# One tile for each PSUM bank of the sums and the scratch, and eight weight blocks halved through PSUM before chunk 1

## The chip, the cores and the metric

The kernel runs on one core of a Trainium2 chip. The metric is the device time of one execution in microseconds (us). The kernel before took 1044.96 us (median of 3 runs, 1044.9 to 1045.19).

## The reference, cut to what matters

Two stages follow each other. The first is a causal convolution over seven taps whose weights are a softmax over the taps, one set for each token and head:

```
w = exp(weight_gen - max(weight_gen)); w = w / (sum(w) + 1e-9)        # [4, 4096, 8, 7]
att[b, s, h, g] = sum over k of w[b, s, h, k] * x_pad[b, s + k, h, g]   # x padded by 6 rows, 8 heads of 24
```

The second is a feed-forward block on the 16384 tokens of 192 numbers:

```
h = att @ w_in                   # [16384, 192] @ [192, 2048]
g = maximum(0.01 * h, h)
out = g @ w_out                  # [16384, 2048] @ [2048, 192]
```

## The kernel before, in words

The tokens are worked in 32 chunks of 512 (four rows of 128 partitions). POOL (GpSimd) does the convolution of a chunk ahead of its use, in 13 multiplications and additions (`conv_ops`, L359 and L363). DVE (VectorE) finds each token's largest value and a power of two for it (`scale_tokens`, L458 to L201), POOL scales by it (L464), and the result is split into a half-precision upper half (ACT, L470) and lower half (POOL, L474). Four DVE transposes (`squares`, L483), a DMA to memory and four back (L490, L500) lay the tokens out as `xx`, the operand of the first product.

A chunk takes eight steps (`step`). In each, TensorE (PE) forms two 128-wide blocks of h (`mm1`, L525, three passes: upper by upper, lower by upper, upper by lower). ACT applies the leak (L531) and takes the upper half `gh` (L545), and DVE takes the lower half `gl` (L546). PE then forms the second product (`mm2_pass`, L571) in two visits: the half of the partitions that goes to one pairing of rows in the same step as the next blocks (`mm2_first`), the other half a step later (`mm2_second`). The blocks of h are numbered n = 0 to 511; step q makes n = 2q and 2q + 1, and PE uses them in step q + 1. The second step of a chunk has no first visit, so the third has four blocks.

PSUM has eight banks. Four go to the blocks of h (`ps_h`). The other four are two tiles of two banks each, tags `o0` and `o1`: in chunks 1 to 31 they are the sums `po`. In chunk 0 and in the first two steps of chunk 1 the tile `o0` is `po0`, the sums of chunk 0 (which are formed in full precision by `mm2_whole`, L611), and `o1` is `spares`, a scratch area that is handed out half by half (`spare`).

The weights arrive in another form, are read and rounded in the beginning, and then have to be scaled and halved in 16 blocks (8 of `w_in`, 8 of `w_out`). There are two ways. Through PSUM: DVE scales into a scratch bank (`v`, L241), ACT copies the upper half (`h`, L249), DVE subtracts (`l`, L253). Straight: ACT scales from SBUF into the upper half (`H`, L258), and DVE scales and subtracts in one instruction on two SBUF operands (`L`, L264). Before, six blocks go through PSUM in the opening, four more through PSUM in steps 8 and 9, and six straight, one in each of steps 10 to 15.

The string `START` is the order written out by hand for the opening, one letter for each piece of work: `f` is a step of chunk 0, `e` one block of its second product, `1`, `2` and `3` the scales of the weights, `D` the sum and division of the softmax for chunks 2 and 3, `y`, `Y`, `X`, `R` the squares and their way through memory, and `v`, `h`, `l`, `H`, `L` the halving. Each engine runs its instructions in the order in which they are issued. DMAs are issued by SP's queue, in order as well. A wait is set by tiles: an instruction that writes a tile waits for those that still read it, whichever part they read.

Of the kernel before, what the change touches and what calls it, by code (L numbers as in the profile page):

```python
# [8 lines left out]
F32 = mybir.dt.float32  # L9
# [5 lines left out]
ALU = mybir.AluOpType  # L15
# [42 lines left out]
    "rWmrWmMppf"  # L58
    "rWmrWmpWmpNeeeef"
    "EBCVmmmmf"  # L60
    "e1De2eyY3eXvhvhlevhlevhlRvhlfvhll"
)


# [1 line left out]
def conv_attention_moe_kernel(  # L66
# [237 lines left out]
    def grouped(q, s):  # L304
        return wt[q][:, s, :].rearrange("p r (h k) -> p (r h) k", k=K)
# [239 lines left out]
        nc.scalar.copy(out=h, in_=t)  # L545
        nc.vector.tensor_tensor(out=l, in0=t, in1=h, op=ALU.subtract)  # L546

    po = [None, None]

    def new_sums():  # L550

        for i in range(2):
            po[i] = ps_o.tile([P, J // 2, TOK], F32, tag=f"o{i}", name="po")

    count = dict(mm2=0)
    after = mybir.DependencyInfo(mybir.DependencyClass.Sync, mybir.DependencyReason.DATA)
# [4 lines left out]
    def mm2_pass(ns, i, told=None):  # L561

        rows = ROWS_OF[::1 if count["mm2"] % 2 else -1]
        for n in ns:
            f = n % NF
            for g, d in ((g_h, 2 * D), (g_l, D)):
                for u, s in enumerate(HALVES):
                    j = rows[(i + u * HALF) % J]  # L570
                    ins = nc.tensor.matmul(  # L571
                        out=po[j // HALF][:, j % HALF, 0:d],
                        lhsT=g[n][s, j * P:(j + 1) * P], rhs=wo[s, f, 0:d],
                        start=(f == 0 and i < HALF and g is g_h),
                        stop=(f == NF - 1 and i >= HALF and g is g_l),
                        skip_group_check=True,
                    ).ins
                    if told is not None:
                        tc.add_manual_dep(ins, told.name, after, reason="rows left")
                        told = None  # L580
        return ins
# [24 lines left out]
    def mm2_whole(ns):  # L606

        for n in ns:
            f = n % NF
            for j in range(J):  # L610
                nc.tensor.matmul(  # L611
                    out=po0[:, j // 2, j % 2 * D:(j % 2 + 1) * D],
                    lhsT=g_h[n][:, j * P:(j + 1) * P], rhs=value((f // 2, OUT))[:, f % 2],
                    start=(f == 0 and j % 2 == 0), stop=(f == NF - 1 and j % 2 == 1),
                    skip_group_check=True,
                )
            del g_h[n]

    def evacuate_whole(c):

        r = row_of(c)
        for k in range(2):
            ot = op.tile([P, HALF, D], F32, tag="ot", name="ot", bufs=2)
            v = po0[:, k, 0:2 * D].rearrange("p (r d) -> p r d", d=D)
            if k:
                nc.vector.tensor_copy(ot, v)
            else:
                nc.scalar.copy(out=ot, in_=v)
            nc.sync.dma_start(out=out_rows[:, r + k * HALF:r + (k + 1) * HALF, :], in_=ot)
# [11 lines left out]
    def evacuate(c, last=False):  # L641


        r = row_of(c)
        for i in range(2):
            k = i if count["mm2"] % 2 else 1 - i
            ot = op.tile([P, HALF, D], F32, tag="ot", name="ot", bufs=2)
            rx = [undo_of[c][:, k * HALF + j:k * HALF + j + 1] for j in range(HALF)]
            for j in range(HALF):
                nc.scalar.activation(  # L650
                    out=ot[:, j], in_=po[k][:, j, D:2 * D], func=AF.Copy, scale=rx[j]
                )
            for j in range(HALF):
                nc.vector.scalar_tensor_tensor(  # L654
                    out=ot[:, j], in0=po[k][:, j, 0:D], scalar=rx[j], in1=ot[:, j],
                    op0=ALU.mult, op1=ALU.add,
                )
            eng = nc.scalar if last and i == 1 else nc.sync
            eng.dma_start(out=out_rows[:, r + k * HALF:r + (k + 1) * HALF, :], in_=ot)
# [31 lines left out]
    with tc.manual_schedule():  # L691
# [44 lines left out]
        def step(q):  # L736

            c, i = divmod(q, NQ)
            if i == 0 and c in sm_q:
                load_weights(sm_q[c])  # L740
                load_rows(sm_q[c])
            if i == 1 and c in sm_q:
                softmax_max(sm_q[c])
                softmax_sub(sm_q[c], nc.gpsimd)
            begun, told = pending.pop() if pending else (None, None)
            mm1(q)
            leak(2 * q)
            if begun:
                mm2_second(begun, told)
                if begun[-1] % NF == NF - 1:  # L750
                    evacuate(begun[-1] // NF)
            split_g(2 * q)
            leak(2 * q + 1)
            split_g(2 * q + 1)
            if q == WHOLE * NQ:
                mm2_whole(range(2 * q - HOLD, 2 * q))
                evacuate_whole(c - 1)
            elif firsts(q):
                ns = firsts(q)
                pending.append((ns, tell(mm2_first(ns))))  # L760
            if c == WHOLE:
                for what in "vhlvhl" if i < 2 else "HL":
                    if done[what.lower()] < len(order):
                        prepare(what)
            if i == 0:
                feed(c + 1, 2 * K)
            if c + 1 < NCH:
                first, turned = TURNS.get(c, (1, 3))
                if i == first:
                    scale_tokens(c + 1)  # L770
                if i == first + 1:
                    split_h(c + 1)
                    split_l(c + 1, nc.gpsimd)
                if i == turned:
                    squares(c + 1, 0)
                    squares(c + 1, 1)
                if i == turned + 1:
                    put_squares(c + 1)
                if i == turned + 2:
                    get_squares(c + 1)  # L780
                if i >= first:
                    feed(c + 2, 1 if c == WHOLE and i == first else 3)
            finish_softmax(c, i)

        po0 = ps_o.tile([P, J // 2, TOK], F32, tag="o0", name="po0")
        spares = ps_o.tile([P, J // 2, TOK], F32, tag="o1", name="spares")
        turn = [0]

        def spare():
            turn[0] += 1  # L790
            if 0 not in xx:
                return po0[:, 1, 0:NW]
            return spares[:, turn[0] % 2, 0:NW]

        w0 = po0[:, 0, 0:J * HK].rearrange("p (h k) -> p h k", k=K)
        away = spares.rearrange("p a b -> p (a b)")
        parts = tiles_of_sets()
        V_G, G_G = slice(0, G0), slice(G0, J * H)
        conv0 = dict(
# [13 lines left out]
        for what in START.replace(" ", ""):  # L813
# [17 lines left out]
            elif what == "a":  # L831
                softmax_max(0, SECOND)
                softmax_sub(0, nc.gpsimd, SECOND)
                softmax_exp(0, SECOND)
            elif what == "b":
                softmax_sum(0, SECOND)
                softmax_div(0, nc.gpsimd, SECOND)
            elif what in conv0:
                run(conv0[what], 1)
            elif what == "Z":  # L840
                heat(HEAT)
            elif what == "t":
                add_transposed(added)
                added += 1
            elif what == "T":
                first_tokens()
            elif what in "123":
                weight_scales("123".index(what))
            elif what == "B":
                scale_tokens(1)  # L850
            elif what == "K":
                load_weights(1)
            elif what == "k":
                load_rows(1)
            elif what == "M":
                softmax_max(1)
            elif what == "N":
                softmax_sub(1, nc.gpsimd)
            elif what == "E":
                softmax_exp(1)  # L860
            elif what == "D":
                softmax_sum(1)
                softmax_div(1, nc.gpsimd)
            elif what == "q":
                feed(2, 1)
            elif what == "C":
                split_h(1)
            elif what == "V":
                split_l(1, nc.gpsimd)
            elif what in "yY":  # L870
                squares(1, "yY".index(what))
            elif what == "X":
                put_squares(1)
            elif what == "R":
                get_squares(1)
            elif what == "f":
                mm1(n)
                leak_out(2 * n)
                leak_out(2 * n + 1)
                n += 1  # L880
            elif what == "e":
                mm2_whole([ended])
                ended += 1
            else:
                raise ValueError(what)
# [37 lines left out]
```

## Time and profile before

| what | value |
|---|---|
| median of 3 runs | 1044.96 us |
| the profiled execution | 1044.78 us |
| its span | 1043.0 us |
| PE busy | 1029.2 us, 99% |
| POOL, ACT, DVE busy | 804.8, 661.8, 565.0 us |
| chain that ended last: PE | 93% |

The span is the time from the first to the last instruction of the execution; 1.78 us lie around it. The chain that ended last is followed back from the last instruction. Time that an engine off that chain is idle costs nothing. A wait of PE, which is busy nearly throughout, is lost time unless the work after it was late anyway. The granted clock is TensorE's, in parts of full speed (1.00 is 2.4 GHz, 0.50 is 1.2 GHz).

### The profile page before, as it was taken

To read this page: it belongs to the slowest core of one execution; us is meant where nothing else is said; L and a number is where in the kernel's file an instruction comes from. 1 tells how busy PE (TensorE), PEld (TensorE's weight loads), DVE (VectorE), ACT (ScalarE), POOL (GpSimd) and SP (SyncE) were. 2 spreads that over 40 slices of the span, in tenths; PEclk is the share of its full clock that TensorE was granted. 3 is DMA by queue.
4 is the path that set the end of the run, shared out by engine and by line. 5 is a ranking of instruction groups with operands and counts; after the bars stand their busy time and mean duration, and the time that the engine had idled before them with its cause. 6 is when DMAs were issued, how large, how long until landed. Compare 5 with 4: busy or idle time off the path is not lost.

```text
span 1043.0 us, 30077 instructions
## 1 busy us (share of the span) xinstructions
PE 1029.2 (99%) x12700; PEld 679.5 (65%) x12700; DVE 565.0 (54%) x1033; ACT 661.8 (63%) x1269; POOL 804.8 (77%) x518
## 2 busy tenths in 40 slices
PE   9979999999999999999999999999999999999998
PEld 6746666666666666666666666666666666666665
DVE  7967455454555554455454555554455454555443
ACT  6547666666666666666666666666666666666664
POOL 7878977779877779877779877779877779987600
PEclk9989999999999999999999999999999999999999
DMA  9431220323222131230323222131230323211120
GB/s 246 144 99 47 87 100 32 109 62 108 62 63 94 47 123 47 76 110 33 108 63 109 62 62 94 47 124 47 84 103 31 109 62 109 63 56 38 47 63 16
DMA packets 42373, 83.06 MB, mean 80 GB/s; under 512 B 4479, under 2 KB 35839, under 8 KB 40446
## 3 DMA queue, kind: packets, MB, share of 16 engines
q1 hardware_dynamic: 42094, 80.95, 25.6%
q8 instruction: 99, 1.62, 0.6%
q14 instruction: 36, 0.29, 0.1%
q10 hardware_dynamic: 144, 0.20, 0.0%
HBM read 56.36 MB, written 24.77 MB: 78 GB/s over the span
## 4 chain that ended last, share of the span: by engine, by line
PE 93%; POOL 3%; DVE 2%; ACT 1%; DMA 1%; issue 0%; SPq 0%; DVEq 0%; POOLq 0%
PE po L571 47%; PE hp L525 46%; POOL acc L363 1%; POOL tmp L359 1%; DMA xx<-far 0%; POOL parts L391 0%; PE po L611 0%; DVE spares L241 0%; DMA far<-sq 0%; ACT hp L531 0%; DVE sm L328 0%; DMA wt<-in_weight_gen_dram 0%; DVE sq L483 0%; DVE most L184 0%; ACT gh L545 0%
## 5 line engine op out<-in xcount | busy, mean ns | idle before, releaser
L546 DVE TENSOR_TENSOR gl<-hp,gh 128x512 f16<-128x512 f32 x496 | 335.6, 686 | 348.2 <-ACT gh L545 344.9
L571 PE MATMUL po<-wo,gh 64*128 64x384 f16 x3968 | 511.7, 323 | 6.1 <-DVE wo L253 6.1
L571 PE MATMUL po<-wo,gl 64*128 64x192 f16 x3968 | 491.2, 243 | 0.4 <-DVE gl L546 0.4
L531 ACT ACTIVATE hp<-hp 128x512 f32<-128x512 f32 x496 | 292.4, 589 | 279.8 <-PE hp L525 279.8
L525 PE MATMUL hp<-xx,wi_h 64*128 64x512 f16 x2976 | 455.8, 377 | 1.0 <-DMA xx<-far 1.0
L363 POOL TENSOR_TENSOR acc<-acc,tmp 128x768 f32<-128x768 f32 x186 | 336.2, 1808 | 14.6
L571 PEld LDWEIGHTS <-gh 64*128 64x128 f16 x3968 | 225.6, 94 | 125.8 <-issue 17.4
L545 ACT CAST gh<-hp 128x512 f16<-128x512 f32 x496 | 291.3, 587 | 15.9 <-PE po L571 1.3
L359 POOL TENSOR_TENSOR tmp<-xt,wt 128x768 f32<-128x768 f32 x186 | 287.8, 1548 | 10.0
L525 PE MATMUL hp<-xx,wi_l 64*128 64x512 f16 x1488 | 295.0, 376 | 0.0
L571 PEld LDWEIGHTS <-gl 64*128 64x128 f16 x3968 | 225.0, 94 | 23.0 <-DVE gl L546 0.8
L525 PEld LDWEIGHTS <-wi_h 64*128 64x128 f16 x2976 | 161.3, 94 | 116.7 <-DMA xx<-far 1.6
L464 POOL TENSOR_TENSOR acc<-acc,xu 128x768 f32<-128x768 f32 x31 | 45.5, 1469 | 145.2 <-DVE xu L201 145.2
L525 PEld LDWEIGHTS <-wi_l 64*128 64x128 f16 x1488 | 84.6, 94 | 76.6 <-issue 0.5
L483 DVE STREAM_TRANSPOSE sq<-split 128x384 f16<-128x384 f16 x124 | 63.8, 553 | 50.5 <-POOL split L474 50.5
L654 DVE SCALAR_TENSOR_TENSOR ot<-po,xr,ot 128x192 f32<-128x192 f32 x124 | 43.2, 410 | 59.9 <-ACT ot L650 59.9
L470 ACT CAST split<-acc 128x768 f16<-128x768 f32 x31 | 25.8, 832 | 48.2 <-POOL acc L464 48.2
L474 POOL TENSOR_TENSOR split<-acc,split 128x768 f16<-128x768 f32 x31 | 51.0, 1645 | 4.7 <-ACT split L470 4.7
L359 POOL TENSOR_TENSOR acc<-xt,wt 128x768 f32<-128x768 f32 x31 | 47.8, 1543 | 0.2
L650 ACT ACTIVATE ot<-po,xr 128x192 f32<-128x192 f32 x124 | 42.2, 421 | 2.6 <-PE po L571 2.6
L458 DVE TENSOR_REDUCE xm<-acc 128x4 f32<-128x768 f32 x31 | 29.2, 943 | 0.3 <-POOL acc L363 0.3
L611 PEld LDWEIGHTS po<-bits,g 128*128 128x128 f32 x128 | 20.6, 190 | 2.7 <-DVE bits L156 0.8
(79 smaller groups left out, 288.3 us busy)
## 6 DMA issues: line engine op xcount, KB each, us to landing
xx<-far SPq DMA_DIRECT2D x124, 192.0 KB, 3.8
xt<-in_x_dram SPq DMA_DIRECT2D x14, 1344.0 KB, 5.9
out_dram<-ot SPq DMA_DIRECT2D x63, 192.0 KB, 1.9
far<-sq SPq DMA_DIRECT2D x31, 384.0 KB, 2.3
wt<-in_weight_gen_dram SPq DMA_DIRECT2D x15, 224.0 KB, 2.6
wi_raw<-in_moe_w_in_dram SPq DMA_DIRECT2D x16, 192.0 KB, 6.4
wo_raw<-in_moe_w_out_dram SPq DMA_DIRECT2D x8, 384.0 KB, 5.7
xt<-in_x_dram SPq DMA_DIRECT2D x2, 384.0 KB, 4.3
```

The source lines that it names most:

```text
L359: eng.tensor_tensor(out=out, in0=tap(c, k), in1=wk, op=ALU.mult)
L363: eng.tensor_tensor(out=acc, in0=acc, in1=out, op=ALU.add)
L464: nc.gpsimd.tensor_tensor(out=att[c], in0=att[c], in1=up.bitcast(F32).to_broadcast([P, J, D]), op=ALU.mult)
L474: eng.tensor_tensor(out=l, in0=att.pop(c), in1=h, op=ALU.subtract)
L483: nc.vector.transpose(out=sq[c][:, v, i], in_=src[:, v])
L525: nc.tensor.matmul(out=hp[2 * q + u], lhsT=w[u][s], rhs=r[s], start=(m == 0), stop=(m == len(passes) - 1),)
L531: return nc.scalar.activation(out=hp[n], in_=hp[n], func=AF.Prelu, alpha=0.01, scale=DOWN).ins
L545: nc.scalar.copy(out=h, in_=t)
L546: nc.vector.tensor_tensor(out=l, in0=t, in1=h, op=ALU.subtract)
L571: ins = nc.tensor.matmul(out=po[j // HALF][:, j % HALF, 0:d], lhsT=g[n][s, j * P:(j + 1) * P], rhs=wo[s, f, 0:d], start=(f == 0 and i < HA ...
L650: nc.scalar.activation(out=ot[:, j], in_=po[k][:, j, D:2 * D], func=AF.Copy, scale=rx[j])
L654: nc.vector.scalar_tensor_tensor(out=ot[:, j], in0=po[k][:, j, 0:D], scalar=rx[j], in1=ot[:, j], op0=ALU.mult, op1=ALU.add,)
```

## The change

Each of the four banks `o0` to `o3` becomes a tile: four tiles of sums, two of chunk 0's sums, two of scratch. The opening halves eight blocks through PSUM, in four groups of two (`vvhhll`), and a ninth straight (`HL`); the steps of chunk 1 halve one block each, straight. The put of the squares (`X`) is issued before a block of chunk 0's second product, and two multiplications of chunk 2's convolution are issued with the letter `q`. In `D` the sum of the softmax and the addition after it go to a scratch bank, and the reciprocal reads it from there.

```diff
-    "e1De2eyY3eXvhvhlevhlevhlRvhlfvhll"
+    "e1De2eyY3Xevvhhllevvhhlle"
+    "RvvhhllfvvhhllqqHL"
...
-    po = [None, None]
+    po = [None] * J
...
-        for i in range(2):
-            po[i] = ps_o.tile([P, J // 2, TOK], F32, tag=f"o{i}", name="po")
+        for j in range(J):
+            po[j] = ps_o.tile([P, TOK], F32, tag=f"o{j}", name="po")
...
-                        out=po[j // HALF][:, j % HALF, 0:d],
+                        out=po[j][:, 0:d],
...
-                    out=ot[:, j], in_=po[k][:, j, D:2 * D], func=AF.Copy, scale=rx[j]
+                    out=ot[:, j], in_=po[k * HALF + j][:, D:2 * D], func=AF.Copy, scale=rx[j]
...
-                for what in "vhlvhl" if i < 2 else "HL":
+                for what in "HL":
...
-        po0 = ps_o.tile([P, J // 2, TOK], F32, tag="o0", name="po0")
-        spares = ps_o.tile([P, J // 2, TOK], F32, tag="o1", name="spares")
+        po0 = [ps_o.tile([P, TOK], F32, tag=f"o{k}", name="po0") for k in range(2)]
+        spares = [ps_o.tile([P, TOK], F32, tag=f"o{k}", name="spares") for k in (2, 3)]
...
-            return spares[:, turn[0] % 2, 0:NW]
+            return spares[turn[0] % 2][:, 0:NW]
...
-                softmax_sum(1)
+                m = spare()[:, 0:R * H].unsqueeze(2)
+                sm[1] = win.tile([P, R * H, 1], F32, tag="sm", name="sm")
+                nc.vector.tensor_reduce(out=m, in_=grouped(1, ALL), axis=AX.X, op=ALU.add)
+                nc.vector.tensor_scalar_add(out=m, in0=m, scalar1=1e-9)
+                nc.vector.reciprocal(out=sm[1], in_=m)
```

Three places show what moves; the lines of the changed kernel are one higher than those of before, and what `D` issues has lines of its own. The first is DVE at `D`, before (`sm` is the softmax's sum, `top` the weights' largest value):

```order
L211 TENSOR_REDUCE both<-most 128x2 [waits DVE_49]
L327 TENSOR_REDUCE sm<-wt 128x64 [waits Activation_49]
L328 TENSOR_SCALAR sm<-sm 128x64 [waits DVE_49]
L329 RECIPROCAL sm<-sm 128x64 [waits DVE_49]
L220 TENSOR_REDUCE top<-spares 1x2 [waits PE_49]
```

The same place now:

```order
L212 TENSOR_REDUCE both<-most 128x2 [waits DVE_49]
L865 TENSOR_REDUCE spares<-wt 128x64 [waits Activation_49]
L866 TENSOR_SCALAR spares<-spares 128x64 [waits DVE_49]
L867 RECIPROCAL sm<-spares 128x64 [waits DVE_49]
L221 TENSOR_REDUCE top<-spares 1x2 [waits PE_49]
```

The order stays, and the addition's operands are in PSUM. The second place is DVE behind the weights' scales, in the opening, before (`wi_l` and `wo` are lower halves):

```order
L228 TENSOR_SCALAR undo<-back 128x1
L241 TENSOR_SCALAR spares<-bits,scale 128x384 [waits DVE_49]
L241 TENSOR_SCALAR spares<-bits,scale 128x384 [waits Activation_49]
L253 TENSOR_TENSOR wi_l<-spares,wi_h 128x384 [waits Activation_49]
L241 TENSOR_SCALAR spares<-bits,scale 128x384 [waits DVE_49]
L253 TENSOR_TENSOR wi_l<-spares,wi_h 128x384 [waits Activation_49]
```

The same place now:

```order
L229 TENSOR_SCALAR undo<-back 128x1
L242 TENSOR_SCALAR spares<-bits,scale 128x384 [waits DVE_49]
L242 TENSOR_SCALAR spares<-bits,scale 128x384
L254 TENSOR_TENSOR wi_l<-spares,wi_h 128x384 [waits Activation_49] x2
L242 TENSOR_SCALAR spares<-bits,scale 128x384 [waits DVE_49] x2
L254 TENSOR_TENSOR wi_l<-spares,wi_h 128x384 [waits Activation_49]
L254 TENSOR_TENSOR wo<-spares,wo 128x2x192 [waits Activation_49]
```

The second scaling no longer waits for ACT's copy of the first, and scalings and subtractions come in twos. The third place is DVE in steps 8 and 9, from the lower halves of step 8 (`gl`) to those of step 9, before:

```order
L546 TENSOR_TENSOR gl<-hp,gh 128x512 [waits Activation_49] x2
L626 COPY ot<-po_114 128x384 [waits Activation_49]
L241 TENSOR_SCALAR spares<-bits,scale 128x384 [waits DVE_49]
L253 TENSOR_TENSOR wi_l<-spares,wi_h 128x384 [waits Activation_49]
L241 TENSOR_SCALAR spares<-bits,scale 128x384 [waits DVE_49]
L253 TENSOR_TENSOR wo<-spares,wo 128x2x192 [waits Activation_49]
L315 TENSOR_REDUCE mx<-wt 128x64 [waits DMAHW4_49]
L546 TENSOR_TENSOR gl<-hp,gh 128x512 [waits Activation_49] x2
```

The same place now, with the straight block of the opening ahead:

```order
L265 SCALAR_TENSOR_TENSOR wi_l<-bits,scale,wi_h 128x384 [waits Activation_49]
L547 TENSOR_TENSOR gl<-hp,gh 128x512 [waits Activation_49] x2
L627 COPY ot<-po_115 128x384 [waits PE_49]
L265 SCALAR_TENSOR_TENSOR wo<-bits,scale,wo 128x2x192 [waits Activation_49]
L316 TENSOR_REDUCE mx<-wt 128x64 [waits DMAHW4_49]
L547 TENSOR_TENSOR gl<-hp,gh 128x512 [waits Activation_49] x2
```

Two blocks through PSUM have become one straight block, and the copy of chunk 0's second half waits for PE alone. POOL's and SP's orders are unchanged.

## Rows read from the trace of the kernel before

**Rows 1.** Waits of PE, whole program: who waited for whom, total us, times, longest.
```profile
PE po L571 <- DVE wo L253: 6.1, 1, 6.1
PE hp L525 <- DMA xx<-far: 1.0, 1, 1.0
```
**Rows 2.** Timeline (start, us, engine, line, [idle before <-releaser]): DVE and PE, 64 to 71.
```profile
66.85 0.69 DVE L546 TENSOR_TENSOR gl<-hp,gh 128x512 f16<-128x512 f32 x1 [0.41 <-ACT gh L545]
...
70.37 0.56 DVE L253 TENSOR_TENSOR wo<-spares,wo 128x384 f16<-128x384 f32 x1 [0.54 <-ACT wo L249]
...
70.98 0.51 PE L571 MATMUL po<-wo,gh 64*128 64x384 f16 x2 [6.05 <-DVE wo L253]
```
**Rows 3.** Chain that ended last, 71 to 82: start, us, what.
```profile
70.98 3.54 PE po L571 x28
74.53 2.79 PE hp L525 x18
77.31 2.94 PE po L571 x48
80.25 1.94 PE hp L525 x18
```
**Rows 4.** Busy time by stretch, with the granted clock behind the engines.
```profile
71.00:74.30 3.30, 3.30 (x29) 2.30 (x30) 2.41 (x4) 2.03 (x4) 0.00 (x0) 0.50 0.00 0
```
**Rows 5.** Timeline at the softmax's sum and the squares of chunk 1.
```profile
43.37 1.64 POOL L474 TENSOR_TENSOR split<-acc,split 128x768 f16<-128x768 f32 x1 [0.94 <-ACT split L470]
43.41 1.65 DVE L328 TENSOR_SCALAR sm<-sm 128x64 f32<-128x64 f32 x1
...
44.36 0.38 PE L214 MATMUL spares<-ident,both 128*1 128x128 f32 x2
...
45.56 0.35 DVE L220 TENSOR_REDUCE top<-spares 1x2 f32<-1x256 f32 x1
...
45.84 1.93 DVE L483 STREAM_TRANSPOSE sq<-split 128x384 f16<-128x384 f16 x4
...
55.78 0.60 PE L525 MATMUL hp<-xx,wi_h 64*128 64x512 f16 x3 [1.05 <-DMA xx<-far]
```
**Rows 6.** Timeline of the halving through PSUM on DVE.
```profile
51.36 0.62 DVE L241 TENSOR_SCALAR spares<-bits,scale 128x384 f32<-128x384 f32 x1
...
52.52 0.56 DVE L253 TENSOR_TENSOR wi_l<-spares,wi_h 128x384 f16<-128x384 f32 x1 [0.54 <-ACT wi_h L249]
...
53.12 0.62 DVE L241 TENSOR_SCALAR spares<-bits,scale 128x384 f32<-128x384 f32 x1
```
**Rows 7.** Timeline of a straight lower half beside POOL; then its line's durations in ns.
```profile
84.77 1.81 POOL L363 TENSOR_TENSOR acc<-acc,tmp 128x768 f32<-128x768 f32 x1
85.36 1.64 DVE L264 SCALAR_TENSOR_TENSOR wi_l<-bits,scale,wi_h 128x384 f16<-128x384 f32 x1
86.66 1.74 POOL L359 TENSOR_TENSOR tmp<-xt,wt 128x768 f32<-128x768 f32 x1
...
L264 DVE SCALAR_TENSOR_TENSOR wo<-bits,scale,wo x4: 609/1335/1634, 80.9 to 96.9; 128x384 f16<-128x384 f32 x4
```
**Rows 8.** Timeline of chunk 2's tokens: POOL and DVE, 65 to 86.
```profile
67.45 1.80 POOL L363 TENSOR_TENSOR acc<-acc,tmp 128x768 f32<-128x768 f32 x1
...
73.72 0.95 DVE L458 TENSOR_REDUCE xm<-acc 128x4 f32<-128x768 f32 x1
...
75.77 1.47 POOL L464 TENSOR_TENSOR acc<-acc,xu 128x768 f32<-128x768 f32 x1 [5.59 <-DVE xu L201]
...
81.55 1.64 POOL L474 TENSOR_TENSOR split<-acc,split 128x768 f16<-128x768 f32 x1 [2.81 <-ACT split L470]
...
83.22 1.04 DVE L483 STREAM_TRANSPOSE sq<-split 128x384 f16<-128x384 f16 x2 [0.68 <-POOL split L474]
```
**Rows 9.** Timeline at the end of chunk 1's sums: DVE's last reading, PE's next writing.
```profile
103.00 1.39 DVE L654 SCALAR_TENSOR_TENSOR ot<-po,xr,ot 128x192 f32<-128x192 f32 x4 [1.71 <-ACT ot L650]
...
104.54 0.34 PE L571 MATMUL po<-wo,gh 64*128 64x384 f16 x2
```

More of the change, by code (lines that the diff above doesn't have):

```diff
@@ L611, in mm2_whole @@
                 nc.tensor.matmul(
-                    out=po0[:, j // 2, j % 2 * D:(j % 2 + 1) * D],
+                    out=po0[j // 2][:, j % 2 * D:(j % 2 + 1) * D],
                     lhsT=g_h[n][:, j * P:(j + 1) * P], rhs=value((f // 2, OUT))[:, f % 2],
@@ L623, in evacuate_whole @@
             ot = op.tile([P, HALF, D], F32, tag="ot", name="ot", bufs=2)
-            v = po0[:, k, 0:2 * D].rearrange("p (r d) -> p r d", d=D)
+            v = po0[k][:, 0:2 * D].rearrange("p (r d) -> p r d", d=D)
             if k:
@@ L654, in evacuate @@
                 nc.vector.scalar_tensor_tensor(
-                    out=ot[:, j], in0=po[k][:, j, 0:D], scalar=rx[j], in1=ot[:, j],
+                    out=ot[:, j], in0=po[k * HALF + j][:, 0:D], scalar=rx[j], in1=ot[:, j],
                     op0=ALU.mult, op1=ALU.add,
@@ L791, in spare @@
             if 0 not in xx:
-                return po0[:, 1, 0:NW]
-            return spares[:, turn[0] % 2, 0:NW]
-        w0 = po0[:, 0, 0:J * HK].rearrange("p (h k) -> p h k", k=K)
-        away = spares.rearrange("p a b -> p (a b)")
+                return po0[1][:, 0:NW]
+            return spares[turn[0] % 2][:, 0:NW]
+        w0 = po0[0][:, 0:J * HK].rearrange("p (h k) -> p h k", k=K)
+        away = spares[0]
         parts = tiles_of_sets()
```

## The prediction

> **What bounds the kernel now.** I read the table of waits of PE first. Over 1043.0 us it holds two waits worth a name: 6.1 us in one piece, until DVE has finished a lower half of a weight block, and 1.0 us until the first tokens of chunk 1 arrive [rows 1]. Elsewhere PE hardly waits, so a faster ACT, DVE or POOL is worth nothing later than these, and the change has to be judged between 43 and about 110 us. The timeline around the long wait shows it to lie between 64.93 (70.98 less 6.05) and 70.98, in the second product of step 10, ended by the subtraction that began at 70.37 [rows 2]. PE has no use for those weights at that point. It has to write the sums of its second pair of rows into the two banks of the scratch tile, and step 9's two blocks still pass through them. The chain that ended last shows the next cost: 28 matmuls take 3.54 us where 48 of the same kind later take 2.94, and a first product takes 2.79 where the next takes 1.94 [rows 3]. The granted clock is 0.50 in this stretch, 1.2 GHz [rows 4]; PE had been idle for 6.05 us just before.
>
> **The change, part by part.**
>
> *The long wait.* The last use of the scratch moves into the opening, ahead of step 8, and only straight blocks follow. What holds PE at 64.93 is gone if the opening is through with the scratch by then. Before, a block costs DVE 1.76 us (53.12 less 51.36 [rows 6]): a scaling of 0.62, a wait of 0.54 for ACT, a subtraction of 0.56. With two banks that are tiles of their own, DVE scales the second block while ACT copies the first, and subtracts the first while ACT copies the second; a pair then costs 2 x 0.62 + 2 x 0.56 = 2.36 and four pairs 9.4. They begin at about 47.6 (below), so the scratch is free at about 57.0, 7 us before PE comes. Saved: 6.05.
>
> *The clock.* Without six idle microseconds I expect the clock to stay at 2.4 GHz. At the rate of the later row (2.94/48 = 0.061) the 28 matmuls take 1.72 instead of 3.54, and the product 1.94 instead of 2.79: 1.82 + 0.85 = 2.67. The first piece includes a little run-in, so I take 2.6. The lower end is 0, if the clock falls for another reason.
>
> *The sum in `D`.* The addition of 64 numbers takes 1.65 us and ends at 45.06, just when POOL's subtraction ends (43.37 + 1.64 = 45.01) [rows 5]: DVE stood still for a port that POOL held. In PSUM the port is not asked for. The time then lies between a sixth of the 0.62 that 384 numbers take [rows 6] and the whole of it; I take 0.2, and even 0.62 would end at 44.0, before the next limit. Behind it come the reciprocal, the reduction at 45.56 and the squares at 45.84. The reduction needs PE's transposes, over at 44.74 (44.36 + 0.38), and takes 0.35, so the squares begin at about 45.1 instead of 45.84. Their way through memory ends with PE's start on chunk 1 at 55.78, after a wait of 1.05 [rows 5]. PE is ready before that, so the shift of 0.75 to 0.8 passes on: I take 0.8. Bounds: 0, if the PSUM form is as slow as before, and 1.05, the whole wait. The weights' scales follow the squares, hence 47.6 for the first halving.
> By the Trainium skill ("SBUF — State Buffer", section "Who interferes with whom") a DVE instruction that reads two SBUF operands or runs in a two-port mode excludes GpSimd from a shared port pair, and whoever issues first holds it to its end. The trace agrees: a straight lower half issued at 85.36 ends at 87.00, 0.42 after the POOL instruction in front, and lasts 1.64 where the shortest lasts 0.61 [rows 7]. The rule speaks for `D` and against the straight blocks: by it every added straight block beside the convolution costs DVE up to 1.03 more, an estimate of 3 us on DVE for the three of steps 8 and 9 and the opening's end; what that does to PE is worked out next from rows alone.
>
> *The straight blocks in steps 8 and 9.* ACT and DVE lose two round trips of 1.76 in each step and get one straight lower half of 0.61 to 1.64 [rows 6, 7]. Of step 9's products the last lower half ended at 67.54 (66.85 + 0.69 [rows 2]). It now ends 0.8 earlier, and by a further 3.52 - 1.64 = 1.88 to 2.91: at 63.8 to 64.9. PE wants it for the last of four blocks of eight matmuls, which start at about 63.9 (64.93 less 4 x 0.061 less 0.8), so at 63.9 + 24 x 0.061 = 65.4. It is there. Cover 0.5 us at worst; cost 0.
>
> *What is late next.* POOL ends chunk 2's convolution at 69.25 [rows 8], and its order does not change. It starts it some 0.7 earlier, because the sum is ready earlier, and each straight block delays POOL: the 1.74 beside the DVE piece holds up to 0.34 of waiting (87.00 less 86.66) [rows 7]. So the convolution ends at about 69.1 whatever PE does. Before, this was no limit: DVE came to it at 73.72, because it was late with the halving, and POOL stood idle for 5.59 us [rows 8]. With PE 9.45 (6.05 + 2.6 + 0.8) ahead DVE arrives first and waits, with the lower halves of step 11 queued behind. From the largest values (73.72) to POOL's scaling (75.77) are 2.05. So POOL scales from 71.1 to 72.6 (1.47), runs one multiplication of at most 1.74 [rows 7] while ACT makes the upper half, and the lower half (1.64 [rows 8]) is done at about 76.0, against 83.19. The squares end 1.04 later, at 77.0, and behind them on DVE stand step 12's two lower halves (0.69 each [rows 2]): 77.7 and 78.4. PE wants them in step 13's second product. From the chain, at full speed, that is 80.25 + 1.94 + 1.96 + 1.94 + 0.98 = 87.1 before [rows 3] (first products of 1.94, second ones of 32 and 16 matmuls of 0.061), so 77.6 now and 78.1 for the second. PE then waits about 0.3. If the straight block of step 11 holds DVE for another 0.6, the wait is 0.9. I take 0.7. The tokens' way through memory stays behind step 13 of PE as before, so it shifts along.
>
> *The four sums' tiles.* In later chunks each bank has its own reader's wait. The last reading of chunk 1's sums ends at 104.39 and PE writes at 104.54 without waiting [rows 9]. I cost it at 0; the cover is 0.15 and is a rival below.
>
> **The sum.** 6.05 + 2.6 + 0.8 - 0.7 = 8.75. The profiled execution took 1044.78 (span 1043.0 and 1.78 around it), 0.18 below the median of the runs shown; 1044.78 - 8.75 = 1036.0, with the median's 0.18 about 1036.2.
>
> **The rivals.**
>
> *Nothing is late next.* POOL's chain comes in time, or DVE gets by without the port: 9.45 gained, 1035.5. For it: the shortfall that I work out is under 1 us, and some of its terms are upper ends (the 1.74, the 2.05). Against: POOL's end at 69.1 stands, and everything behind it is one wait after the other. 0.22.
>
> *The cover is thinner.* The pairs in the opening do not overlap: eight blocks at 1.76 take 14.1 instead of 9.4, and all that DVE and ACT do after it comes 4.7 later. Step 9's last lower half then ends at up to 64.9 + 4.7 = 69.6, PE waits up to 4.2, and the gain is 8.75 - 4.2 = 4.5: 1040.4; with half of that delay 1038.3. POOL's chain can do the same if convolution and straight blocks hold each other up by 2 us more. For it: ACT's copies and DVE's pieces have hardly any play in a pair (0.54 of waiting against 0.56 and 0.62 of work [rows 6]). Against: nothing in the order makes the second scaling wait for ACT. 0.20.
>
> *It does not do what it says.* The sums still wait for the scratch, since a wait is set by tile and the new ones share tags with the old. Then only the 0.8 of the start remains: 1044.2. Against: the last reader of each scratch bank stands in front of step 8 now. 0.06, within measurement.
>
> *Slower: the sums' banks at chunk ends.* ACT's and DVE's readings come bank by bank, each with its own wait on PE. If an evacuation were pushed back by two of ACT's readings, some 0.7 us, DVE's last reading would end 0.55 after PE needs the bank (0.7 less 0.15), at each of the 30 ends of chunks 1 to 30: 16.5 lost against 8.75, 1052.7. It decides from a delay of 0.44 on (8.75/30 + 0.15). For it: 0.15 is little. Against: both banks of a pair get their last products within one pass, so the second wait ends with the first. 0.04.
>
> **How the numbers follow.** The forecast has 0.48 and the rivals 0.22, 0.20, 0.06 and 0.04. A measurement of this kernel can tell about 0.2% from no change, 2.1 us. The forecast and the first two rivals are all faster by more: 0.90. The third is within it: 0.06. The last is slower: 0.04. The range runs from 1034.9 (all gained, and 0.6 for the open 0.25 in `D` and the clock's run-in) to 1040.0, nearly all of the thinner cover.
>
> **What would show it.** Right: in PE's waits the one on a lower half of the weights is gone and none above 1 us stands in its place; the granted clock is 1.00 from 60 to 80 us; the addition in `D` takes about 0.2, the squares begin at about 45.1 and PE's first product with arrived tokens at about 55.0; DVE waits for POOL's last accumulation before chunk 2's largest values, which it never did before; straight lower halves in steps 8 and 9 last over 1 us. Wrong: PE idle for more than 2 us between 60 and 90 us; a clock of 0.50 there; a wait of PE on a reading of the sums at a chunk's end; or later chunks that take longer than before.

## The result, and the profile after

The changed kernel takes 1033.14 us (median of 5 runs, 1033.01 to 1033.66); the kernel before took 1044.96 in the same session (5 runs, 1044.81 to 1045.37). The ratio is 0.9887, interval 0.9872 to 0.9901: faster by 11.8 us. I had forecast 1036.2, a gain of 8.75, and a range that began at 1034.9. The profiled execution went from a span of 1043.0 to 1031.3, so 11.7 are to be accounted for. (The helpers that the change adds lines to move by one: L571 of before is L572 of after, and so on.)

The table of waits of PE, without the run-in (who waited for whom, total us, times, longest). In place of the 6.1 and 1.0 of [rows 1]:

```profile
PE hp L526 <- DMA xx<-far: 0.4, 1, 0.4
PE po L572 <- DVE gl L547: 0.4, 1, 0.4
```

The long wait is gone. The 0.4 on DVE does not stand in its place: it lies in the last product of the program (1024.74), where the kernel before has it too (1036.18). The busy time by stretch, in place of [rows 4], shows the clock (behind the engines, before the DMA share):

```profile
60.00:80.00 20.00, 19.85 (x245) 11.23 (x246) 15.97 (x24) 15.09 (x28) 18.39 (x12) 1.00 0.11 41
71.00:74.30 3.30, 3.30 (x44) 1.95 (x42) 2.81 (x4) 1.75 (x3) 2.81 (x2) 1.00 0.03 7
```

It is 1.00, 2.4 GHz, where it was 0.50, and PE puts 44 matmuls (of both products) into the 3.3 us that held 29. The timeline at the softmax's sum and the squares answers to [rows 5], and two rows to the halving of [rows 6]:

```profile
43.39 1.64 POOL L475 TENSOR_TENSOR split<-acc,split 128x768 f16<-128x768 f32 x1 [0.94 <-ACT split L471]
43.44 0.23 DVE L866 TENSOR_SCALAR spares<-spares 128x64 f32<-128x64 f32 x1
...
45.17 1.93 DVE L484 STREAM_TRANSPOSE sq<-split 128x384 f16<-128x384 f16 x4
...
47.65 1.14 DVE L242 TENSOR_SCALAR spares<-bits,scale 128x384 f32<-128x384 f32 x2
...
49.80 1.13 DVE L242 TENSOR_SCALAR spares<-bits,scale 128x384 f32<-128x384 f32 x2
...
55.20 0.60 PE L526 MATMUL hp<-xx,wi_h 64*128 64x512 f16 x3 [0.42 <-DMA xx<-far]
```

The addition takes 0.23 instead of 1.65 beside the same POOL instruction, the squares begin 0.67 earlier, PE begins chunk 1 at 55.20 instead of 55.78, and two blocks cost DVE 2.15 (49.80 less 47.65). The fourth pair takes 2.98 (54.11 to 57.09), since DVE waits 0.91 for ACT in it; the four together take 9.44. Chunk 2's tokens answer to [rows 8]:

```profile
67.30 1.81 POOL L364 TENSOR_TENSOR acc<-acc,tmp 128x768 f32<-128x768 f32 x1
67.86 1.66 DVE L265 SCALAR_TENSOR_TENSOR wo<-bits,scale,wo 128x384 f16<-128x384 f32 x1
69.45 0.94 DVE L459 TENSOR_REDUCE xm<-acc 128x4 f32<-128x768 f32 x1
...
71.49 1.47 POOL L465 TENSOR_TENSOR acc<-acc,xu 128x768 f32<-128x768 f32 x1 [1.14 <-DVE xu L202]
...
74.74 1.63 POOL L475 TENSOR_TENSOR split<-acc,split 128x768 f16<-128x768 f32 x1
...
76.41 1.04 DVE L484 STREAM_TRANSPOSE sq<-split 128x384 f16<-128x384 f16 x2 [1.51 <-POOL split L475]
77.37 1.25 DVE L547 TENSOR_TENSOR gl<-hp,gh 128x512 f16<-128x512 f32 x2
...
78.07 0.10 PEld L572 LDWEIGHTS <-gl 64*128 64x128 f16 x2 [0.45 <-DVE gl L547]
...
78.67 0.10 PEld L572 LDWEIGHTS <-gl 64*128 64x128 f16 x2 [0.24 <-DVE gl L547]
```

POOL's idle time ahead of its scaling shrank from 5.59 to 1.14, and DVE now waits 1.51 for POOL ahead of the second squares, with two lower halves behind it. The weight loads (PEld) that need these two wait 0.45 and 0.24 for them, and PE's second product there takes 2.38 (76.63 to 79.01) instead of 1.96: 0.42 is lost, and PE's table of waits does not show it. DVE does not wait for POOL ahead of the largest values: POOL's convolution ends at 69.11 (67.30 + 1.81), and step 10's straight lower half in front of them only at 69.52.

The straight lower halves answer to [rows 7] (ns, shortest, median, longest):

```profile
L265 DVE SCALAR_TENSOR_TENSOR wo<-bits,scale,wo x5: 694/1600/1661, 60.6 to 84.1; 128x384 f16<-128x384 f32 x5
L265 DVE SCALAR_TENSOR_TENSOR wi_l<-bits,scale,wi_h x3: 681/1259/1317, 57.1 to 72.1; 128x384 f16<-128x384 f32 x3
```

Most last over 1 us, and PE waits for no lower half of the weights. The one of step 10 stands in the chain to the 0.42 all the same: it took 0.61 before (at 73.19) and takes 1.66 now, beside POOL.

All that was in the forecast. The rest of the gain is at the chunk ends, where [rows 9] had seemed to show nothing. First the timeline after, ACT and PE's weight loads included:

```profile
93.36 1.35 ACT L651 ACTIVATE ot<-po,xr 128x192 f32<-128x192 f32 x4
...
93.81 1.39 DVE L655 SCALAR_TENSOR_TENSOR ot<-po,xr,ot 128x192 f32<-128x192 f32 x4 [1.83 <-ACT ot L651]
...
95.37 0.10 PEld L572 LDWEIGHTS <-gh 64*128 64x128 f16 x2
95.59 0.33 PE L572 MATMUL po<-wo,gh 64*128 64x384 f16 x2
```

Then the rows of before around the two in [rows 9] that I had not read:

```profile
102.24 1.36 ACT L650 ACTIVATE ot<-po,xr 128x192 f32<-128x192 f32 x4
...
104.51 0.12 PEld L571 LDWEIGHTS <-gh 64*128 64x128 f16 x2 [0.38 <-issue]
```

Before, DVE began its four readings 0.76 after ACT's four (103.00 less 102.24); now 0.45 (93.81 less 93.36). Before, DVE's last one ended at 104.39 and the first weight load of the next sums came at 104.51, after 0.38 of idle time that the profile puts down to nothing ("issue"); its matmul began 0.03 behind it. Now the load is there 0.22 ahead of its matmul (95.59 less 95.37). The chain shows the price. Of before and of after, the first second product of the new sums in chunk 2, then the rows of 48 matmuls of the first and the last whole chunk:

```profile
104.63 2.05 PE po L571 x32
...
108.62 2.94 PE po L571 x48
...
1016.49 2.94 PE po L571 x48
```

```profile
95.75 1.96 PE po L572 x32
...
99.65 2.94 PE po L572 x48
...
1005.03 2.94 PE po L572 x48
```

The product takes 1.96 instead of 2.05, and there are 29 chunks between the two rows of 48: (1016.49 - 108.62) / 29 = 31.306 before, (1005.03 - 99.65) / 29 = 31.220 after, 0.086 less each. The account: 8.97 by the first of these rows (108.62 - 99.65; it holds one chunk end), 2.49 over 29 chunks, and 0.24 behind the last of them, where DVE's very last reading begins 0.46 after ACT's instead of 0.76. Together 11.70. Without its one chunk end the first term is 8.88; I had forecast 8.75 for it.

The loads' sum over the program had shown this before too (busy, mean ns of one | idle before, and what ended it), of before and after:

```profile
L571 PEld LDWEIGHTS <-gh 64*128 64x128 f16 x3968 | 225.6, 94 | 125.8 <-issue 17.4 <-ACT gh L545 0.2 <-SPq L585 0.2
```

```profile
L572 PEld LDWEIGHTS <-gh 64*128 64x128 f16 x3968 | 193.1, 94 | 142.1 <-ACT gh L546 0.2 <-SPq L586 0.2
```

17.4 of "issue", of which some 6.2 are the long wait; the other 11.2 are 30 ends of 0.37. After, there is none.

### The profile page after: what moved, and what is told of

The parts are those of the page before. It is cut to its first block, busy times and chain, and to the rows that moved or that the text cites. A ratio compares the mean times of both kernels' runs of the same rounds, so it can differ in the third digit from the quotient of the medians.

```text
span 1031.3 us, 30034 instructions
## 1 busy us (share of the span) xinstructions
PE 1024.4 (99%) x12700; PEld 613.6 (60%) x12700; DVE 565.9 (55%) x1031; ACT 661.0 (64%) x1269; POOL 805.7 (78%) x518
## 4 chain that ended last, share of the span: by engine, by line
PE 95%; POOL 1%; DVE 1%; DMA 1%; ACT 1%; issue 0%; SPq 0%; DVEq 0%; POOLq 0%
PE hp L526 48%; PE po L572 46%; PE po L612 1%; DMA xx<-far 0%; ACT hp L532 0%; POOL parts L392 0%; DVE sq L484 0%; DMA far<-sq 0%; DMA wt<-in_weight_gen_dram 0%; DVE gl L547 0%; ACT gh L546 0%; POOL acc L360 0%; POOL split L475 0%; POOL parts L395 0%; DVE wo L265 0%
## 5 line engine op out<-in xcount | busy, mean ns | idle before, releaser
L572 PE MATMUL po<-wo,gh 64*128 64x384 f16 x3968 | 506.4, 323 | 0.0
L572 PE MATMUL po<-wo,gl 64*128 64x192 f16 x3968 | 486.4, 243 | 0.5 <-DVE gl L547 0.4
L526 PE MATMUL hp<-xx,wi_h 64*128 64x512 f16 x2976 | 443.3, 376 | 0.4 <-DMA xx<-far 0.4
L526 PE MATMUL hp<-xx,wi_l 64*128 64x512 f16 x1488 | 282.9, 376 | 0.0
L572 PEld LDWEIGHTS <-gh 64*128 64x128 f16 x3968 | 193.1, 94 | 142.1 <-ACT gh L546 0.2
L526 PEld LDWEIGHTS <-wi_h 64*128 64x128 f16 x2976 | 141.3, 94 | 135.3 <-DMA xx<-far 1.1
L572 PEld LDWEIGHTS <-gl 64*128 64x128 f16 x3968 | 193.1, 94 | 30.8 <-DVE gl L547 1.5
L526 PEld LDWEIGHTS <-wi_l 64*128 64x128 f16 x1488 | 72.7, 94 | 88.2
L612 PE MATMUL po<-bits,g 128*128 128x192 f32 x128 | 22.3, 330 | 0.0
```

Of the source, the lines that this page charges most:

```text
L526: nc.tensor.matmul(out=hp[2 * q + u], lhsT=w[u][s], rhs=r[s], start=(m == 0), stop=(m == len(passes) - 1),)
L572: ins = nc.tensor.matmul(out=po[j][:, 0:d], lhsT=g[n][s, j * P:(j + 1) * P], rhs=wo[s, f, 0:d], start=(f == 0 and i < HALF and g is g_h), ...
```

## The experiments

Theory, once the trace was read: before, DVE's first reading of two sums waited for ACT's second one, because both sums were one tile; so DVE's last reading ended too late for the next chunk's first weight load, at each of 30 ends. Rivals: it is the number or the place of the load's waits that costs, not the lateness (at the loads' line the kernel before has 30 semaphore instructions of 51 ns, one for each end, and the changed kernel none); or the order of the opening changed something that lasts.

**The banks alone.** Before, with only the part of the diff that makes each bank a tile (all the edits of `po`, `po0` and `spares`).

```
-            po[i] = ps_o.tile([P, J // 2, TOK], F32, tag=f"o{i}", name="po")
+            po[j] = ps_o.tile([P, TOK], F32, tag=f"o{j}", name="po")
...
```

> The kernel before with the four bank tiles (sums, chunk 0's sums, scratch) and nothing else: the order of the opening and the sum in D as before. My theory now: the gain that I missed belongs to the tiles, 0.086 us at each of 30 chunk ends (31.306 less 31.220 us a chunk) and 0.3 at the last reading, and the long wait stays, since step 9's blocks still use the scratch: 2.6 + 0.3 = 2.9 gained, 1042.1, chunks of 31.22. Rival (the chunks got shorter by the order, for instance because POOL's work lies otherwise from step 10 on): chunks stay at 31.306, 1044.7.

Measured 1040.8 (5 runs, 1040.38 to 1041.47), ratio 0.9961 [0.9948, 0.9973]. The loads' row:

```profile
L571 PEld LDWEIGHTS <-gh 64*128 64x128 f16 x3968 | 215.0, 94 | 127.0 <-issue 5.4 <-ACT gh L545 0.2 <-SPq L585 0.2
```

The loads' unexplained idle time falls to the long wait alone (PE's table of waits has 5.3 for it), the rows of 48 matmuls stand 31.22 apart, and the last DVE reading begins 0.45 after ACT's. So DVE waited by the tile of sums although it only reads it; by the data it needs ACT's first reading and no more. More was gained than expected: the row of 48 in chunk 2 comes 1.36 earlier (107.26 against 108.62). One chunk end is 0.09 of it, the long wait ends 0.55 earlier (70.43), and the first product behind it takes 2.07 instead of 2.79, with a mean granted clock of 0.74 from 72 to 76 us where it was 0.50.

**The order alone.** Before, with two-bank tiles but the new `START`, the straight blocks in steps 8 and 9, and the sum in PSUM.

```
+    "e1De2eyY3Xevvhhllevvhhlle"
+    "RvvhhllfvvhhllqqHL"
...
-                for what in "vhlvhl" if i < 2 else "HL":
+                for what in "HL":
...
```

> The kernel before with the new order of the opening and of the steps and the new D, but the tiles of two banks. My theory: the long wait (6.05) and the slow clock (2.6) go and D's 0.6 comes, about 0.4 to 1 is lost again to chunk 2's tokens, and the chunks stay at 31.306 with the last reading as before: 1036.1 to 1036.8. Pairs no longer overlap (the second scaling waits for the first copy), 2.9 us a pair instead of 2.3. Rival (the order shortens the chunks): 1033 to 1034.

Measured 1040.06 (5 runs, 1039.06 to 1040.96), ratio 0.9952 [0.9939, 0.9964]. The chunk ends are as before, as expected; the loads' row:

```profile
L572 PEld LDWEIGHTS <-gh 64*128 64x128 f16 x3968 | 224.6, 94 | 119.5 <-issue 11.3 <-ACT gh L546 0.2 <-SPq L586 0.2
```

11.3 are again 30 ends of 0.38, and chunks take 31.306. But the kernel is some 3.5 slower than I expected of it: the order needs the banks too. The timeline of DVE at `D`:

```profile
45.99 0.63 DVE L865 TENSOR_REDUCE spares<-wt 128x64 f32<-128x448 f32 x1 [2.38 <-PE spares L215]
```

The sum in `D` has to wait 2.38 for PE's transposes into the other half of the same tile, where in the changed kernel it stood at 42.78; and two blocks of the opening take 3.26 (their scalings begin at 56.77 and 60.03 for the last two pairs) instead of 2.15, DVE waiting 0.93 for ACT in each pair. So the two parts of the change are not independent: a scratch in use by halves is only two scratches once its halves are two tiles. This run's opening was also about 1 us late with its input.

**Shorter readings.** Before, with DVE's readings of the sums cut from 192 to 64 columns; the other 128 columns of the output lack one part of their sum.

```
-                    out=ot[:, j], in0=po[k][:, j, 0:D], scalar=rx[j], in1=ot[:, j],
+                    out=ot[:, j, 0:64], in0=po[k][:, j, 0:64], scalar=rx[j], in1=ot[:, j, 0:64],
...
```

> The kernel before, with DVE's last reading of the sums cut to 64 of 192 columns, so that it ends some 0.5 us earlier (the other 128 columns of the output lack one part of the sum). Theory of lateness: PE's first weight load of the new sums waits for the end of that reading, 104.39 in the trace of before, so the 0.086 at each chunk end goes although tiles and waits are as before: chunks of 31.22, 2.6 less, and another 0.2 to 0.5 at the very end: 1041.9 to 1042.2. Rival theory of place: the two waits on the weight load cost 0.086 whether or not they are met; chunks stay at 31.306, 1044.5 to 1044.8.

Measured 1042.44 (8 runs, 1041.08 to 1042.7), ratio 0.9974 [0.9964, 0.9984]. The chunk end, DVE and PE's load and matmul:

```profile
103.44 1.10 DVE L654 SCALAR_TENSOR_TENSOR ot<-po,xr,ot 128x64 f32<-128x64 f32 x4 [1.71 <-ACT ot L650]
...
104.68 0.11 PEld L571 LDWEIGHTS <-gh 64*128 64x128 f16 x2
104.89 0.34 PE L571 MATMUL po<-wo,gh 64*128 64x384 f16 x2
```

The semaphore instructions at the loads' line (ns; first and last start in us) are the 30 of before:

```profile
L571 PEldq EVENT_SEMAPHORE  x30: 51/51/51, 104.6 to 1010.0; - x30
```

DVE still begins 0.77 after ACT (102.67 in this run), but ends 0.14 ahead of the load (103.44 + 1.10 = 104.54), and the load is again 0.21 ahead of its matmul. ACT's readings of the first and the last whole chunk begin at 102.67 and 1008.05: (1008.05 - 102.67) / 29 = 31.22. (The total is 0.24 above the range that I expected; in the profiled run the first of these readings came 0.43 later than before.) With nothing but 0.29 us less of DVE's work the loss is gone, tiles and waits as before. The lateness is the cause.

**More waits.** The changed kernel, with waits added to that load that have long been met.

```
+                    if f == 0 and i == 0 and u == 0 and g is g_h and last_read:
+                        for d_ in last_read + last_sum:
+                            tc.add_manual_dep(ins, d_.name, after, reason="again")
...
```

> The changed kernel with dependencies added that are met long before: the first matmul of each chunk's sums also waits for ACT's last reading and PE's last writing of the old sums. At 15 of the 30 chunk ends this puts a second wait on the weight load, as before the change; at the other 15 nothing is added. Theory of place: 0.086 at 15 ends, 1.3 us: 1034.4, every second chunk at 31.306. Theory of lateness: nothing, 1033.1, all chunks at 31.22.

Measured 1033.2 (4 runs, 1033.03 to 1033.41), ratio 0.9889 [0.9874, 0.9904]; chunks stay at 31.22. The semaphore instructions at the loads' line, of which the changed kernel has none:

```profile
L573 PEldq EVENT_SEMAPHORE  x15: 51/51/51, 95.2 to 969.4; - x15
```

The waits are there, at 15 ends, and they cost nothing once they have been met.

**In turn.** The changed kernel, with DVE's first reading of two sums made to wait for ACT's second one again.

```
+                if j == 0:
+                    tc.add_manual_dep(both_, read.name, after, reason="in turn")
...
```

> The changed kernel, but DVE's first reading of a pair of sums waits until ACT has read both banks of the pair, as it had to when the two banks were one tile. Theory: the chunk ends cost 0.086 each because DVE's last reading came 0.3 later behind ACT's and the next chunk's first weight load stood behind it. Then chunks take 31.22 plus 0.03 to 0.09 again and the end of the program is 0.3 later: 1034.3 to 1036.0. Rival: not the readers' order but which semaphores the weight load waits on makes the difference: chunks stay at 31.22, and only the end of the program is up to 0.3 later: 1033.1 to 1033.5.

Measured 1034.65 (4 runs, 1034.57 to 1036.32), ratio 0.9903 [0.9889, 0.9918]. DVE and the first load of the next sums, at the ends of chunks 1 and 2 (ACT's readings begin at 93.34 and 124.63):

```profile
94.11 1.39 DVE L655 SCALAR_TENSOR_TENSOR ot<-po,xr,ot 128x192 f32<-128x192 f32 x4 [2.14 <-ACT ot L651]
...
95.62 0.12 PEld L572 LDWEIGHTS <-gh 64*128 64x128 f16 x2 [0.38 <-issue]
...
125.39 1.39 DVE L655 SCALAR_TENSOR_TENSOR ot<-po,xr,ot 128x192 f32<-128x192 f32 x4 [1.61 <-ACT ot L651]
...
126.65 0.28 PEld L572 LDWEIGHTS <-gh 64*128 64x128 f16 x2
```

DVE is 0.76 to 0.77 behind ACT at both ends, but the load is held at the first only. The rows of 48 matmuls follow at 31.22 and 31.30 by turns:

```profile
99.73 2.94 PE po L572 x48
...
130.95 2.94 PE po L572 x48
...
162.25 2.94 PE po L572 x48
...
193.47 2.94 PE po L572 x48
```

The "issue" of the loads is 5.6, 15 ends of 0.37. `mm2_pass` takes its rows forwards and backwards by turns (`ROWS_OF[::1 ... -1]`): the next chunk's first matmul writes now the bank that DVE read last, now the one it read first. So the change helps at the ends twice over: each bank having its own reader's wait saves half of them by itself, and DVE ending 0.3 earlier saves all of them, as the short readings showed. In the changed kernel none is left.

**The sum in SBUF.** The changed kernel, with the sum of `D` as before.

```
-                m = spare()[:, 0:R * H].unsqueeze(2)
...
+                softmax_sum(1)
```

> The changed kernel, but `D` makes its sum as before (addition and reduction through SBUF instead of a PSUM bank). Theory: the port costs the start on chunk 1 what the trace of the changed kernel gained there, 0.58: the addition of 64 numbers takes about 1.6 instead of 0.23, the squares begin at about 45.8 instead of 45.17, PE's first product on chunk 1 at about 55.8 instead of 55.20, and everything behind shifts, PE's wait of 0.4 for DVE at chunk 2 included, since POOL also starts 0.6 later. 1033.1 + 0.6 = 1033.7. Rival: the start on chunk 1 is set by DMAs alone and the sum's place is worth nothing: 1033.1, with PE's wait for the tokens larger or smaller by what the squares move.

Measured 1033.89 (4 runs, 1033.85 to 1033.95), ratio 0.9892 [0.9878, 0.9907]. The timeline of the addition and of PE's start on chunk 1:

```profile
43.49 1.65 DVE L329 TENSOR_SCALAR sm<-sm 128x64 f32<-128x64 f32 x1
...
55.96 0.60 PE L526 MATMUL hp<-xx,wi_h 64*128 64x512 f16 x3 [1.12 <-DMA xx<-far]
```

The addition takes 1.65 again and PE's wait for tokens goes from 0.42 to 1.12: 0.7 for the sum's place, at the start on chunk 1. In the total this can't be told with certainty, since the changed kernel itself came out at 1033.75 in another session (below); the rows tell it.

**No pairs.** The changed kernel, with the opening's blocks taken one by one.

```
-    "e1De2eyY3Xevvhhllevvhhlle"
-    "RvvhhllfvvhhllqqHL"
+    "e1De2eyY3Xevhlvhlevhlvhle"
+    "RvhlvhlfvhlvhlqqHL"
```

> The changed kernel, but the eight blocks of the opening are taken one by one (scale, upper, lower) instead of in pairs. This is what my prediction's rival 'the cover is thinner' describes. Theory: DVE waits 0.54 for ACT in every block, a block takes 1.76 and two 3.52 instead of the measured 2.15 a pair, so DVE leaves the opening's halving 5.5 later (4 x 1.37). It can make up about 2 of that where it waited for POOL before chunk 2's largest values (1.5 and 0.9). PE then waits between 1 and 5 us for lower halves between 57 and 75: 1034 to 1038, most likely 1036.5. Rival: the banks alone make the blocks overlap, since the next scaling goes to the other bank and DVE's order doesn't matter: two blocks still 2.2 to 2.5, no wait, 1033.1 to 1033.5.

Measured 1034.67 (4 runs, 1034.57 to 1036.63), ratio 0.9906 [0.9889, 0.9923]. The start of the first and the last scaling, and where PE pays:

```profile
47.63 0.62 DVE L242 TENSOR_SCALAR spares<-bits,scale 128x384 f32<-128x384 f32 x1
...
59.12 0.61 DVE L242 TENSOR_SCALAR spares<-bits,scale 128x384 f32<-128x384 f32 x1
...
63.74 0.59 PE L526 MATMUL hp<-xx,wi_h 64*128 64x512 f16 x3 [0.74 <-DVE gl L547]
```

Eight blocks at (59.12 - 47.63) / 7 = 1.64: DVE is through the eight at 60.79 instead of 57.09, 3.7 later, and PE loses 0.9 in waits and 1.5 by the row of 48 matmuls (101.19 against 99.65). The time is 1.8 below the one that I had called most likely. It is the order of the letters, not the banks alone, that makes two blocks overlap. My rival had put the loss at 2 to 4: PE's cover was about 2 us (3.7 less 1.5), not the 0.5 that I had worked out.

**Against the two waits left.** The changed kernel, with the first of step 12's two lower halves ahead of the second squares of chunk 2, and the first squares ahead of the weights' maximum (`START` "e1Dey2e...").

```
+            if c == WHOLE and i == TURNS[c][1] + 1:
+                squares(c + 1, 1)
...
-                    squares(c + 1, 1)
+                    if c != WHOLE:
+                        squares(c + 1, 1)
```

> The changed kernel with two moves against its two remaining waits in the chain: step 12's last lower half is issued on DVE ahead of the squares of chunk 2 (PE waited 0.39 for it), and in the opening DVE makes the first squares ahead of the weights' maximum (in the chain of the changed kernel that maximum's 0.41 stands ahead of them). Theory: both are links of the chain that ends last, so they come off: up to 0.39 and up to 0.4, 1032.3 to 1032.7. Rival: the squares of chunk 2 that come 0.7 later delay the tokens' way through memory, and PE then waits for tokens what it no longer waits for weights; the scales that come 0.4 later are likewise paid back by a later lower half: 1033.1.

Measured 1033.67 (4 runs, 1033.2 to 1034.41), ratio 0.9891 [0.9876, 0.9906]: nothing won, though not in the way of my rival. The 0.39 of the theory was misread: it is the wait at the end of the program, and what chunk 2 loses is 0.42. The edit also moves the first of the two lower halves, not the last; the second still stands behind the squares, and the second product still takes 2.18 instead of 1.96. PE no longer waits for the tokens of chunk 1. Its table holds two waits on DVE, 0.8 together: the one at the end and a new one. The timeline of the new one:

```profile
107.88 1.04 DVE L484 STREAM_TRANSPOSE sq<-split 128x384 f16<-128x384 f16 x2 [1.78 <-POOL split L475]
...
109.55 0.26 PE L572 MATMUL po<-wo,gl 64*128 64x192 f16 x2 [0.36 <-DVE gl L547]
```

The first row of 48 matmuls comes 0.39 earlier (99.26), 0.18 by the tokens and 0.2 by the lower half; the next comes 31.87 later instead of 31.22. POOL sets the date of chunk 3's squares as it did of chunk 2's, and a PE that is earlier waits there.

**Squares later still.** The first of these two edits, with chunk 3's squares a step later; the same with the second edit too; and the changed kernel again beside them.

```
-TURNS = {1: (2, 3)}
+TURNS = {1: (2, 3), 2: (1, 4)}
```

> The changed kernel; step 12's last lower half is issued ahead of the second squares of chunk 2, and the squares of chunk 3 are issued a whole step (3.9 us) later. In the kernel with only the first of these (and an earlier first maximum in the opening) PE won 0.39 at chunk 2 and then waited 0.65 for a lower half that stood on DVE behind chunk 3's squares, which waited for POOL. Theory: POOL's work on the first chunks is the next limit, and with chunk 3's squares out of the way of the lower halves too PE waits for neither: 0.39 gained, 1032.7. Rival: POOL's lateness is passed on by another way (the tokens of chunk 3 come too late, or DVE's lower halves meet the squares one step later): 1033.1 or more.

> As the one before, and in the opening DVE makes the first squares ahead of the weights' maximum, which took PE's wait of 0.4 for the tokens of chunk 1 away in the earlier trial. Theory: 0.39 and 0.4 come off, 1032.3. Rival: as before, 1033.1 or more.

> The changed kernel once more, beside the two below, so that tenths of a microsecond can be compared within one session: 1033.1, within 0.3.

Measured 1036.42 (4 runs, 1035.25 to 1036.94), ratio 0.9917 [0.9904, 0.9931]; 1036.82 (5 runs, 1035.37 to 1037.6), ratio 0.9922 [0.991, 0.9935]; and 1033.75 (4 runs, 1033.27 to 1034.19), ratio 0.9895 [0.9879, 0.991]. The rival was right: the chain of the first of them goes through the tokens of chunk 3. (Both theories count on the misread 0.39.)

```profile
117.05 4.39 DMA xx<-far
...
121.49 2.06 PE hp L526 x17
```

PE waits for the transfer that a step's delay made late (0.66 and 1.40 in its timeline). No version that I tried beats the changed kernel. Its own median moved by 0.6 between sessions with no edit, so a difference of that size between two sessions says nothing; where I tell tenths above, they are read from rows.

## Why the prediction was wrong

*The step that failed:* "The four sums' tiles. ... I cost it at 0; the cover is 0.15", and before it "Elsewhere PE hardly waits, so a faster ACT, DVE or POOL is worth nothing later than these". I compared the end of DVE's last reading with PE's next matmul and took 0.15 for play. The instruction that has to wait is the weight load ahead of that matmul, and it stood 0.12 behind DVE's end, held by it: a load that is not held comes 0.21 to 0.22 ahead of its matmul, and this one came 0.03 ahead. The wait of 0.38 was in the table of loads, named "issue", and not in PE's table of waits, which I had read first and believed. The term is 30 ends of 0.086, 2.58, and the same early start of DVE gives 0.24 at the last reading. The other sign of the same place was my rival of slower; I looked at what the new tiles could add and not at what the old tile was costing.

What DVE's 0.76 meant could have been seen as well. By the Trainium skill ("PSUM — Partial Sum Buffer", section "PSUM bank collisions raise a hardware error") two engines must not be in one bank, in the same partitions, at the same time, two readers included; it advises a guard by bank and quarter of the partitions, or more simply by bank. The trace agrees in the order of the readings: with bank tiles DVE follows ACT by 0.45, about one of ACT's readings (0.42 each, the mean of 124), and with tiles of two banks it followed by 0.76, about two of them (0.73 in the last pair, where they stand alone). No run here lets two engines into one bank at once.

*The long wait, 6.05, and the clock, 2.6.* Right: chunk 1's pass of 48 matmuls begins at 67.84 instead of 77.14, 9.30 earlier; less the start's 0.58 the two gave 8.72, that is 6.05 and 2.67, and the granted clock is 1.00 from 60 to 80 us.

*The sum in `D`, 0.8.* The mechanism was right (0.23 against an expected 0.2; 1.65 again when put back), the size 0.58, because the squares began 0.67 earlier and not 0.74 to 0.8, and the tokens' transfer took 4.32 where it had taken 4.24.

*The straight blocks, 0.* PE waits for no lower half of the weights, as I said, and their durations, 0.68 to 1.66, are those expected from [rows 7] (of the two that I had named as over 1 us, step 8's takes 1.50 and step 9's 0.68); the cover was larger than I had worked out.

*What is late next, 0.7.* Right in its place, and 0.42 in size, but one link was another. POOL's convolution ended at 69.11 (69.1 expected), but DVE came to chunk 2's largest values only behind step 10's straight lower half, at 69.45. The sign that I had named for this, a wait of DVE for POOL there, did not come. From there on the links held: the second squares ended at 77.45 (77.0 expected). No run takes that straight block out, so what share of the 0.42 is its own is not shown.

*The pairs in the opening.* Three of 2.15 each and one of 2.98 (2.36 expected), 9.44 in all against 9.4; that the sum fits so well is luck.

So the early part is 6.05 + 2.67 + 0.58 - 0.42 = 8.88 against 8.75, from terms that each missed by about 0.3 or less, and of the 2.95 by which the profiled gain of 11.70 was missed 2.82 is one term that I had put at 0.

## What to carry to other kernels

Where TensorE seems to wait for nothing, read its weight loads too: a small idle time without a name, at the same place in every turn of a long loop, multiplies by the turns. The 0.42 that PE loses at chunk 2 is seen there too, and not in PE's table of waits, where a 0.4 of another place stands. A tile of several PSUM banks makes every wait on one bank a wait on all, for readers behind readers as well as for the writer behind them, so the order of use and the tiles have to be chosen together: here either alone gave 4 to 5 of 11.8. And when the engine on the bound gets ahead, the next one that sets dates (POOL here) is late at the next place of the same kind, so a fix there only moves the wait by one turn.

## What was not expected of the hardware

A weight load that is held costs less than it waits: 0.37 to 0.38 of idle time in the loads' row, 0.086 in PE's, since the load normally stands 0.21 to 0.22 ahead of its matmul, and here 0.03. And the profile names no one for it, although the wait is on DVE: with 0.29 less of DVE's work it is gone.
